# Spectral mixer and gated FFN on one core: T stored in another row order, one transfer where there were two, later T stores spread over more steps, down sums one unit later, modulation rows in pieces

## The chip, the cores and the metric

The kernel runs on one core of a Trainium2 chip. A core has a matrix engine (TensorE, PE in the profile; its weight loads are PEld), VectorE (DVE), ScalarE (ACT), GpSimd (POOL), and SyncE (SP), whose queue issues the transfers between the memory off the core (DRAM here) and the core's own memory of 128 partitions. The transfers themselves are carried by 16 DMA engines. Each engine works through its own instructions in program order and waits on semaphores for the others. The metric is device time in microseconds, from the program's start to its end; lower is better.

## The reference

One block with adaptive layer norm around a spectral mixer (A) and a gated FFN (B), for 8192 tokens of 448 channels in float32. Cut to what matters:

```
sa, ca, ga, sb, cb, gb = (silu(c) @ w_mod) in six rows of 448
h = layernorm(x) * (1 + ca) + sa
z = rfft2(h, over the 8192 tokens)               # complex, in 4 blocks of 112 channels
h = relu(z @ w1 + b1)                            # complex product, per block
o = softshrink(h @ w2 + b2, 0.01)                # complex product, per block
x = x + ga * irfft2(o)
h = layernorm(x) * (1 + cb) + sb
x = x + gb * ((gelu(h @ w_gate) * (h @ w_up)) @ w_down)
```

## The kernel before

The 8192 tokens are taken as 128 by 64, and the transform is done as two short ones. Three parts follow each other.

**Stage A** (lines 130 to 400): x is loaded in 16 pieces `xt` of four columns each, normalised and transformed along the 128 (`dft_a`, L213). The result T, 128 rows (64 frequencies, real and imaginary) by 64 columns by 448 channels, replaces x in `xt` (`out_a`, L218). `store_t` (L355) writes it to DRAM as `td`. The order of the 128 rows is set by the columns of the transform's matrix (`cols` in `_consts`); partition p of `xt` holds the row whose place in a list of four groups (c, 0 to 3) is given by p modulo 4. Pieces 0 to 3 (below `CE`) are stored whole; of pieces 4 to 15 the group c = 0 is stored in stage A, and the 36 remaining stores (the list `late`) are issued during the next stage. `td` has the row order of the partitions, so the four frequencies of a unit lie some rows apart.

**Units** (`step`, L640 on): 32 units, each of four frequencies (`GB`) and half of the channels (224, `HC`). Step i does six things for different units, so that the engines overlap: `fetch_t` loads T of unit i+2 into one of two buffers `tr` (L427: one transfer for the real and one for the imaginary rows, each with 64 columns on the partitions); `stage_s2` does the second transform of unit i on PE (L461 to L463) and ACT and DVE split its result in two f16 parts, `zh` and `zl`; `split_t` splits T of unit i+1 on POOL (`th`, `tl`); `stage_m2`, `stage_m1` are the two products of units i-2 and i-1; `split_y` makes `yh` (ACT) and `yl` (POOL) of unit i-2; `stage_i1` does the first inverse transform of unit i-3 and copies it into one of two buffers `us` (L590), which `store_us` (L607) writes to DRAM as `vd` in two transfers, real and imaginary part. The first two units are fetched by `fetch_first` (columns 0 to 59, from `td`) and `fetch_last` (the last four columns, straight from `xt`, eight transfers of 7 KB). Units 8 and 9 hold frequency 0 and need extra work on POOL, DVE and PE.

Beside this the steps carry work for the FFN, placed by calls of `at(step, hook, ...)`: `load_w` loads 14 pieces of w_gate and w_up into the buffers of `xt` that are free by then (L806: 384 rows; L808: the last 64 rows, twice, onto both halves of the partitions), `squares`, `norms` use them; `load_m`, `down_max`, `down_sums` (POOL, L953 to L956), `store_sums` do seven pieces of w_down; `row_scales` scales the modulation rows. The hooks of a step are called in the order load, pe, act, dve, pool. All transfers are issued by SP in the order in which the program calls them; a transfer that has to wait holds back those behind it.

Ahead of the first unit, `mod_cols`, `dc_cols`, `scale_of` and `mod_row` (L244) turn the modulation into scaled weights w1 and w2.

**FFN** (L970 on): the rest of the inverse transform, read back from `vd` (`load_v`), and the three products of B; nothing there is edited.

The lines that set the two transfers of a unit's result:

```
r = bt * 2 * GB
for ro in range(2):
    dma(vd[h, :, r + ro * GB : r + (ro + 1) * GB], us[ro * 64 : ro * 64 + 64])
```

Of the kernel before, what the change touches and what calls it, by code (L numbers as in the profile page):

```python
# [19 lines left out]
D = 448  # L20
F = 1792
NA, NB, NG = 128, 64, 64
# [28 lines left out]
def spectral_geglu(ctx, tc, x, w1, b1, w2, b2, wg, wu, wd, cvec, wmod, cf1, cs2, cmi, cgm, out):  # L51
# [92 lines left out]
    with ExitStack() as actx:  # L144
# [89 lines left out]
            else:  # L234
                V.scalar_tensor_tensor(ms[:, c], wm[:, k, c], cs[:, k : k + 1], ms[:, c], op0=ALU.mult, op1=ALU.add)

        def mod_row(h, then=lambda: None):

            r = (sb_r, cb_r)[h]
            ps = bank("pd", "psm")  # L240
            for k in range(4):
                if k == 2:
                    then()
                T.matmul(  # L244
                    ps[:, :D], cs[:, k : k + 1].to_broadcast([112, 128]), wn[:, k, h * D : (h + 1) * D], start=k == 0, stop=k == 3
                )
            return lambda: S.copy(r, ps[:, :D])

        ca1 = lp.tile([113, NBLK], F32, name="ca1")
        sa0 = lp.tile([112, NBLK], F32, name="sa0")  # L250
# [100 lines left out]

        def store_t(ch, c=None):

            r = slice(0, 128) if c is None else slice(c, 128, NC)
            dma(td[r, ch * 4 : ch * 4 + 4], xts[ch][r])  # L355


        plan = []
# [43 lines left out]
    with ExitStack() as bctx:  # L402
# [1 line left out]

        tts, trs = {}, {}

        def rows(ri, bt):
            r = BTS.index(bt) * 2 * GB + ri * GB
            p = r % (128 // NC) * NC + r * NC // 128
            return slice(p, p + (GB - 1) * NC + 1, NC)  # L410

        s2s = {}

        def fetch_first(h, ri):
            n = NB - 4
            dma(
                trs[units[h]][0][ri * 64 : ri * 64 + n],
                td[rows(ri, BTS[0]), :n, h * HC : (h + 1) * HC].rearrange("g b c -> b g c"),
            )

        def fetch_last(h, b):
            dma(trs[units[h]][0][NB - 4 + b : 128 : 64], xts[NB // 4 - 1][0 : 2 * GB * NC : NC, b, h * HC : (h + 1) * HC])

        def fetch_t(h, bt):
            raw = bp1.tile([128, GB, HC], F32, tag="tr", name="tr", bufs=2)
            for ri in range(2) if (h, bt) not in units[:2] else ():
                dma(  # L427
                    raw[ri * 64 : ri * 64 + 64],
                    td[rows(ri, bt), :, h * HC : (h + 1) * HC].rearrange("g b c -> b g c"),
                )  # L430
# [53 lines left out]
        def stage_m1(h, bt):  # L484
            zs = ctx_u.pop(("z", h, bt))
            hs = []
            kr = 113
            w = ZW if bt == 0 else GB * 64
            for kk in range(2):
                k = 2 * h + kk  # L490
                zhi, zlo = zs[kk]
                if bt == 0:
                    banks = [bank("pb", "pm1a")[:BS, :w], bank(("pa", "pd")[kk], "pm1b")[:BS, :w]]
                else:
                    ps = bank("pb", "pm1")
# [12 lines left out]
                cnt["h"] += 1  # L508
                hlo = bp.tile([BS, 2, ZW], F16, tag="hl", name="hl", bufs=4)
                if bt == 0:  # L510
                    for ro in range(2):
                        S.activation(hhi[:BS, ro, :w], banks[ro], AF.Relu)
                        V.scalar_tensor_tensor(
                            hlo[:, ro, :w], banks[ro], 0.0, hhi[:BS, ro, :w], op0=ALU.max, op1=ALU.subtract
                        )
                    for ro in range(2):
                        h0 = bp.tile([BS, 1], F32, tag="h0", name="h0", bufs=2)
                        j = slice(ro * NBLK + k, ro * NBLK + k + 1)
                        V.tensor_scalar(h0, banks[ro][:, 0:1], hb[:, j], 0.0, op0=ALU.add, op1=ALU.max)
# [21 lines left out]
        def stage_m2(h, bt, p):  # L541
# [17 lines left out]
            drip()  # L559
            if bt == 0 and p == 0:  # L560

                pn = bank("pb", "pn")
# [39 lines left out]
        def store_us(h, bt, us=None):  # L602

            us = late_us[h, bt] if us is None else us
            r = bt * 2 * GB
            for ro in range(2):
                dma(vd[h, :, r + ro * GB : r + (ro + 1) * GB], us[ro * 64 : ro * 64 + 64])  # L607


        tiny = []  # L610
# [30 lines left out]
        def step(i):  # L641
# [9 lines left out]
            hook("pe")  # L651
            if 1 <= i and i + 1 < nu:
                split_t(*units[i + 1])
            m2 = 0 <= i - 2 < nu
            if m2:
                y = [stage_m2(*units[i - 2], p) for p in range(2)]
# [6 lines left out]
            hook("dve")  # L663
            if 0 <= i - 3 < nu:
                stage_i1(*units[i - 3])
            hook("pool")

        def m2_i1(i, j, el=G):

# [33 lines left out]
        ctx.enter_context(tc.manual_schedule())  # L703
        for u in units[:2]:
            fetch_t(*u)
        for h in range(2):
            for ri in range(2):
                fetch_first(h, ri)
        for h in range(2):
            for b in range(4):  # L710
                fetch_last(h, b)
        zh = [bp1.tile([113, 2, ZW], F16, name=f"zh{i}") for i in range(4)]
        hh_ = [bp1.tile([113, 2, ZW], F16, name=f"hh{i}") for i in range(4)]
        mod_cols()
        bounds1()
        for z in zh:
            S.activation(z[96:113, 0], ones[96:113], AF.Copy, scale=2.0**-ZSC)
        for z in hh_:
            G.tensor_copy(z[96:113, 0], ones[96:113])
        hb_out = dc_cols()  # L720
        scale_of(0, 4, modulated)
        bounds2()
        hb_out()
        weights1()
        row_copy = mod_row(0, lambda: scale_of(1, 13))
        weights2_hi()
        row_copy()
        row_copy = mod_row(1)

        late = [(ch, c) for ch in range(CE, NB // 4) for c in range(1, NC)]  # L730

        def store_late(n):
            for ch, c in late[:n]:
                store_t(ch, c)
            del late[:n]

        store_late(6)

        for u in units[:2]:
            split_t(*u, el=V)  # L740
        row_copy()
# [61 lines left out]
        def load_w(pool, pr, j):  # L803
            wsrc = (wg, wu)[pr][:, j * 256 : (j + 1) * 256]
            raw = raw_tile(pool)
            dma(raw[:, 0:3, :], wsrc[0:384].rearrange("(t p) f -> p t f", p=128))  # L806
            for hh in range(2):
                dma(raw[hh * 64 : hh * 64 + 64, 3, :], wsrc[384:448])  # L808
            return raw

        def squares(pr, j, el=S):
# [151 lines left out]
        for n, i in enumerate([3, 4, 5, 6, 7, 8, 9, 10, 11, 11, 12, 12, 13, 14]):  # L963
            j, pr = divmod(n, 2)
            at(i, "load", pre, npool, ("n", pr, j), load_w, pr, j)
            at(i + 1, "act", squares, pr, j, V if i in (3, 5, 7, 11, 12) and (i < 11 or pr) else S)
            at(i + 2, "pe", norms, pr, j)
            at(i + 2, "pe", norms_out, pr, j)
        for j, i in enumerate([4, 6, 8, 9, 10, 13, 14]):
            at(i, "load", pre, npool, ("m", j), load_m, j)  # L970
            at(i + 1, "dve", down_max, j)
            at(i + 1, "pool", down_sums, j)
            at(i + 2, "load", store_sums, j)
        at(11, "dve", row_scales)
        at(16, "pe", scales1)
        at(16, "pe", scales2)
        for i in range(6):
            at(i, "load", store_late, 5)
        at(1, "act", thresholds)
        for i in range(17):  # L980
            step(i)
# [993 lines left out]
def _consts():  # L1975
# [34 lines left out]
    s2 = s2.reshape(64, 128, 128).transpose(1, 0, 2) * 2.0 ** SSC  # L2010
    s2h = s2.astype(np.float16)
    s2l = (s2 - s2h).astype(np.float16)
    cols = [ri * 64 + bt + NBT * j for bt in BTS for ri in range(2) for j in range(GB)]
    cols = np.array(cols).reshape(NC, 128 // NC).T.reshape(-1)
    rows = np.zeros((128, 2))
    rows[:112, 0], rows[112, 1] = 1, 2.0**-ZSC
# [33 lines left out]
```

## Time and profile before

| | us |
|---|---|
| median of 3 runs (lowest, highest) | 1871.42 (1870.48, 1872.85) |
| the profiled execution | 1873.0 |
| its span in the trace | 1871.0 |
| first matmul of unit 0 (L461) | 81.07 |
| first matmul of unit 31 | 331.90 |
| first and last copy into `us` (L590) start at | 106.1, 354.4 |

In the trace's groups over the stretch 81 to 225 us, the group of DVE's squares (L817) has 5 instructions with a mean of 1435 ns, the group of ACT's squares (L815) 9 with 1048 ns. From step to step the first matmul of a unit comes every 7.5 to 8.2 us, but for steps 9, 10, 11, 13 and 20, which take 13.4, 11.4, 10.0, 10.6 and 10.0 us (from 145.13, 158.54, 169.95, 187.75 and 245.99 us); from 272 us on it is 7.5 us every time. A row of the timeline gives start, length, engine, line, operation and, in brackets, how long the engine sat idle before it and for whom. The table by stretches gives for each stretch the busy time of each engine with its count of instructions, the clock granted to PE, the mean busy share of the 16 DMA engines, and what they moved. The view of the transfers gives the same share in 40 slices, the packets by size, the share of each queue and, below, the transfers issued in the stretch, with KB each.

### The profile page before, as it was taken

How to read it: one execution, taken by the hardware profiler on the slowest of the kernel's cores; microseconds unless marked ns; L12 is line 12 of the kernel's file. 1: busy time of each engine (PE TensorE's matmuls, PEld its weight loads, DVE VectorE, ACT ScalarE, POOL GpSimd, SP SyncE). 2: the span in 40 equal slices, each digit the busy share in tenths (PEclk: the TensorE clock that was granted, in tenths of full speed). 3: DMA queues.
4: the chain of work that ended last, by engine and by line, in shares of the span. 5: the costliest groups of instructions: out<-in, count | busy, mean ns of one | idle time of the engine just before them, and what ended most of it. 6: DMA issues, size and time to landing. Idle time of an engine off the chain costs nothing.

```text
span 1871.0 us, 56475 instructions
## 1 busy us (share of the span) xinstructions
PE 1824.1 (97%) x23352; PEld 1727.0 (92%) x23352; DVE 1415.3 (76%) x2914; ACT 968.4 (52%) x1815; POOL 1318.4 (70%) x1724
## 2 busy tenths in 40 slices
PE   7998999899999999999999999999999999999998
PEld 3697989778898988999999999999999999999998
DVE  8698999887766667777777777777777777777745
ACT  5665678643444444455555555555545554444443
POOL 3377878257777778777777777777777777777534
PEclk9899999999999999999999999999999999999999
DMA  9898878664444445966666666666666666666551
GB/s 355 297 317 235 223 196 226 204 144 104 104 104 104 104 104 124 293 170 170 169 170 169 170 170 170 172 178 178 173 170 172 177 177 177 170 175 174 161 160 55
DMA packets 380613, 330.48 MB, mean 177 GB/s; under 512 B 110784, under 2 KB 358724, under 8 KB 380356
## 3 DMA queue, kind: packets, MB, share of 16 engines
q1 hardware_dynamic: 380356, 326.87, 64.0%
q8 instruction: 183, 3.00, 0.7%
q14 instruction: 74, 0.61, 0.1%
HBM read 243.26 MB, written 60.10 MB: 162 GB/s over the span
## 4 chain that ended last, share of the span: by engine, by line
PE 84%; DVE 5%; DMA 4%; POOL 2%; ACT 2%; issue 1%; SPq 1%; ACTq 0%; POOLq 0%; DVEq 0%
PE set L1485 39%; PE pgu L1242 11%; PE pdn L1315 6%; PE pdn L1317 6%; PE pdn L1316 6%; PE ps L213 2%; PE set L1315 2%; PE set L1317 2%; PE set L1316 2%; DVE y L556 1%; DMA vd<-us 1%; POOL tl L117 1%; POOL yl L117 1%; DMA tr<-td 1%; PE set L1609 1%
## 5 line engine op out<-in xcount | busy, mean ns | idle before, releaser
L1485 PE MATMUL set<-nt,wk 128*128 128x128 f16 x13104 | 736.4, 219 | 3.1 <-ACT sb L1513 1.5
L1485 PEld LDWEIGHTS <-wk 128*128 128x128 f16 x13104 | 733.9, 98 | 3.5 <-issue 2.3
L1317 PE MATMUL pdn<-wd,ac 128*128 128x224 f16 x1218 | 315.5, 259 | 0.6 <-DVE ac L1303 0.6
L1315 PE MATMUL pdn<-wd,ac 128*128 128x224 f16 x1218 | 315.7, 259 | 0.0
L1316 PE MATMUL pdn<-wd,ac 128*128 128x224 f16 x1218 | 315.5, 259 | 0.0
L1242 PE MATMUL pgu<-nt,wk 128*128 128x256 f16 (+1 forms) x2464 | 269.7, 274 | 4.8 <-DVE x L1283 4.8
L1242 PEld LDWEIGHTS <-wk 128*128 128x128 f16 (+1 forms) x2464 | 226.4, 98 | 46.8 <-issue 20.3
L1534 ACT ACTIVATE gl<-c,dg 128x384 f32<-128x384 f32 x168 | 103.5, 616 | 230.2 <-DVE c L1528 227.3
L1560 DVE SCALAR_TENSOR_TENSOR ac<-x,sa_act,ac 128x896 f16<-128x896 f32 x168 | 205.5, 1223 | 20.1 <-ACT ac L1550 20.0
L1291 POOL TENSOR_TENSOR x<-x 128x128 f32<-128x128 f32 x223 | 131.2, 589 | 121.8 <-DVE x L1283 60.9
L1361 POOL TENSOR_TENSOR cq<-cq 128x224 f32<-128x224 f32 x32 | 21.1, 659 | 262.5 <-DVE cq L1360 262.5
L1292 POOL TENSOR_TENSOR x<-x 128x128 f32<-128x128 f32 x223 | 186.4, 836 | 17.5
L1550 ACT ACTIVATE ac<-x,sa_act 128x896 f16<-128x896 f32 x168 | 174.2, 1037 | 14.7 <-POOL x L1294 7.9
L1538 DVE TENSOR_TENSOR x<-c,gl 128x384 f32<-128x384 f32 x168 | 153.3, 912 | 17.2 <-ACT gl L1534 17.0
L1315 PEld LDWEIGHTS <-ac 128*128 128x128 f16 x1568 | 153.4, 98 | 4.9 <-issue 4.8
L1317 PEld LDWEIGHTS <-ac 128*128 128x128 f16 x1568 | 153.4, 98 | 0.8 <-DVE ac L1303 0.8
L1316 PEld LDWEIGHTS <-ac 128*128 128x128 f16 x1568 | 153.5, 98 | 0.1
L1522 DVE TENSOR_TENSOR c<-set,sb 128x512 f32<-128x512 f32 x168 | 115.3, 686 | 35.7 <-PE set L1485 35.6
L1278 ACT ACTIVATE gel<-pgu,dg 128x256 f32<-128x256 f32 x112 | 49.4, 470 | 159.5 <-PE pgu L1242 151.8
L1293 POOL TENSOR_TENSOR x<-x 128x128 f32<-128x128 f32 x223 | 131.7, 591 | 0.0
L1513 ACT COPY sb<-set 128x512 f32<-128x512 f32 x168 | 97.4, 580 | 62.0 <-PE set L1485 60.7
L1294 POOL TENSOR_TENSOR x<-x 128x128 f32<-128x128 f32 x223 | 126.3, 566 | 0.0
(348 smaller groups left out, 3892.3 us busy)
## 6 DMA issues: line engine op xcount, KB each, us to landing
wk<-wk SPq DMA_DIRECT2D x76, 1024.0 KB
wk<-wk SPq DMA_DIRECT2D x76, 768.0 KB
vd<-us SPq DMA_DIRECT2D x64, 224.0 KB
xx<-in_A_x SPq DMA_DIRECT2D x32, 448.0 KB
v<-vd SPq DMA_DIRECT2D x63, 224.0 KB
out<-x SPq DMA_DIRECT2D x31, 448.0 KB
xt<-in_A_x SPq DMA_DIRECT2D x15, 896.0 KB
tr<-td SPq DMA_DIRECT2D x60, 224.0 KB
```

The lines of the kernel that those rows point to most:

```text
L1242: T.matmul(pgu[i, t, q][:, pr * H : (pr + 1) * H], ws[rows, n, w, tw], nts[i][rows, tn, :], start=start, stop=stop, skip_group_check=True,)
L1291: e.tensor_tensor(s1, a21, a22, ALU.add)
L1292: e.tensor_tensor(s2, s1, a11, ALU.subtract)
L1293: e.tensor_tensor(s3, a11, a21, ALU.subtract)
L1294: e.tensor_tensor(s4, a12, s2, ALU.subtract)
L1315: T.matmul(ps, ac[:, 0, ka], w[:, 0, kb], start=n == 0, stop=False)
L1316: T.matmul(ps, ac[:, 0, ka], w[:, 1, kb], start=False, stop=False)
L1317: T.matmul(ps, ac[:, 1, ka], w[:, 0, kb], start=False, stop=n == NP - 1)
L1485: T.matmul(ps2[:, pr, reg * 128 : reg * 128 + 128], slot[:, pr, hl, wt, :], nt[:, xt, :], start=start and j == 0, stop=j == len(terms) - 1 ...
L1538: V.tensor_tensor(xs[u][:, 1::3, :], cts.pop(u)[:, 1], gls.pop(u), ALU.mult)
L1550: S.activation(ac[:, 0], xs[u][:, 0:7], AF.Copy, scale=sa_act[:, t : t + 1])
L1560: V.scalar_tensor_tensor(ac[:, 1], xs.pop(u)[:, 0:7], sa_act[:, t : t + 1], ac[:, 0], op0=ALU.mult, op1=ALU.subtract)
```

## The change

- `cols`: the rows of T stand in another order, frequency by frequency with real and imaginary part side by side, and `store_t` writes `td` in that order (a whole piece as 32 x 4 x 1792, a group as 32 rows in a row). A unit's eight rows then lie together, and `fetch_t` is one transfer of 128 partitions (columns and real or imaginary part) for every unit, the first two too; `rows`, `fetch_first`, `fetch_last` go.
- `store_us` and the last rows of `load_w` are one transfer each instead of two. The destination of the first and the source of the second have a leading dimension of two.
- The 36 later stores of T: three to five in each of the steps 0 to 5 and two or three in steps 6 to 10, instead of six ahead of the units and five in each of the steps 0 to 5; their order is changed so that group c = 1 comes in time.
- `mod_row` takes the pieces k that it is to do; `scale_of(0)` comes ahead of `dc_cols`.
- `down_sums` stands one step later and ahead of `split_y` instead of at the step's end; `store_sums` one step later; `row_scales` at step 13 instead of 11; three of the squares move from DVE to ACT.
- The banks of PSUM of unit 8 and 9's first product change places (`pa`, `pd`), and `pn` takes one of `pd`.

```diff
+        rps = {}
+        def mod_row(h, ks):
+            if h not in rps:
+                rps[h] = bank("pd", "psm")
+            for k in ks:
                 T.matmul(
-                    ps[:, :D], cs[:, k : k + 1].to_broadcast([112, 128]), wn[:, k, h * D : (h + 1) * D], start=k == 0, stop=k == 3
+                    rps[h][:, :D], cs[:, k : k + 1].to_broadcast([112, 128]), wn[:, k, h * D : (h + 1) * D], start=k == 0, stop=k == 3
                 )
...
         def store_t(ch, c=None):
-            r = slice(0, 128) if c is None else slice(c, 128, NC)
-            dma(td[r, ch * 4 : ch * 4 + 4], xts[ch][r])
+            b = slice(ch * 4, ch * 4 + 4)
+            if c is None:
+                dma(td[:, b].rearrange("(c m) b e -> m c b e", c=NC), xts[ch])
+            else:
+                dma(td[c * (128 // NC) : (c + 1) * (128 // NC), b], xts[ch][c:128:NC])
...
-            for ri in range(2) if (h, bt) not in units[:2] else ():
-                dma(
-                    raw[ri * 64 : ri * 64 + 64],
-                    td[rows(ri, bt), :, h * HC : (h + 1) * HC].rearrange("g b c -> b g c"),
-                )
+            r = BTS.index(bt) * 2 * GB
+            dma(raw, td[r : r + 2 * GB, :, h * HC : (h + 1) * HC].rearrange("(g o) b c -> (o b) g c", o=2))
...
-                    banks = [bank("pb", "pm1a")[:BS, :w], bank(("pa", "pd")[kk], "pm1b")[:BS, :w]]
+                    banks = [bank("pb", "pm1a")[:BS, :w], bank(("pd", "pa")[kk], "pm1b")[:BS, :w]]
...
-            for ro in range(2):
-                dma(vd[h, :, r + ro * GB : r + (ro + 1) * GB], us[ro * 64 : ro * 64 + 64])
+            dma(vd[h, :, r : r + 2 * GB].rearrange("b (o g) c -> o b g c", o=2), us)
...
                 split_t(*units[i + 1])
+            hook("pool")
             m2 = 0 <= i - 2 < nu
...
                 stage_i1(*units[i - 3])
-            hook("pool")
...
-        for h in range(2):
-            for ri in range(2):
-                fetch_first(h, ri)
-        for h in range(2):
-            for b in range(4):
-                fetch_last(h, b)
...
-        late = [(ch, c) for ch in range(CE, NB // 4) for c in range(1, NC)]
+        n = NB // 4
+        late = [(ch, c) for ch in range(CE, n - 6) for c in range(1, NC)] + [(ch, 1) for ch in range(n - 6, n)]
+        late += [(ch, c) for ch in range(n - 6, n) for c in range(2, NC)]
...
-        store_late(6)
...
-            for hh in range(2):
-                dma(raw[hh * 64 : hh * 64 + 64, 3, :], wsrc[384:448])
+            dma(raw[:, 3, :], wsrc[384:448].rearrange("(o p) f -> o p f", o=1).to_broadcast([2, 64, 256]))
...
-            at(i + 1, "act", squares, pr, j, V if i in (3, 5, 7, 11, 12) and (i < 11 or pr) else S)
+            at(i + 1, "act", squares, pr, j, V if i in (11, 12) and pr else S)
...
-            at(i + 1, "pool", down_sums, j)
-            at(i + 2, "load", store_sums, j)
-        at(11, "dve", row_scales)
+            at(i + 2, "pool", down_sums, j)
+            at(*((i + 3, "load") if i + 3 < 17 else (16, "dve")), store_sums, j)
+        at(13, "dve", row_scales)
...
-        for i in range(6):
-            at(i, "load", store_late, 5)
+        for i, n in enumerate([3, 4, 4, 4, 5, 5, 2, 2, 2, 2, 3]):
+            at(i, "load", store_late, n)
...
-    cols = [ri * 64 + bt + NBT * j for bt in BTS for ri in range(2) for j in range(GB)]
+    cols = [ri * 64 + bt + NBT * j for bt in BTS for j in range(GB) for ri in range(2)]
```

On SP, from the end of step 3 to the loads of step 4, the transfers stand as follows before the change (destination, source, and the size of the destination's dimensions; `td` are late stores of T, `vd` a unit's result, `tr` the fetch, `s` a constant, `xt` buffers that now take weights):

```order
L355 DMA td<-xt_139 32x1792 x3
L355 DMA td<-xt_140 32x1792 x2
L607 DMA vd<-us 64x896 x2
L427 DMA tr<-td 64x4x224 x2
L435 DMA s_1309<-cs 128x1024
L806 DMA xt_133<-in_B_w_up 128x3x256
L808 DMA xt_133<-in_B_w_up 64x256 x2
L938 DMA xt_134<-in_B_w_down 128x2x448
```

And after it:

```order
L360 DMA td<-xt_135 32x1792
L360 DMA td<-xt_136 32x1792 x3
L593 DMA vd<-us 2x64x896
L417 DMA tr<-td 128x4x224
L422 DMA s_1281<-cs 128x1024
L788 DMA xt_133<-in_B_w_up 128x3x256
L789 DMA xt_133<-in_B_w_up 128x1x256
L919 DMA xt_134<-in_B_w_down 128x2x448
```

Three pairs became single transfers: the fetch with 128 outermost on both sides, the result's store with a 2 ahead of the 64 in the destination (its source has 128 partitions), and the weights' last rows, whose source is 2 x 64 x 256 with a step of 0 in the first dimension.

On POOL, from `split_y` in step 4 to `split_t` in step 6, the first of the down sums (`xt_134`) stands like this before:

```order
L117 TENSOR_TENSOR yl<-y,yh 128x448 x2
L115 CAST th<-tr 128x896
L117 TENSOR_TENSOR tl<-tr,th 128x896
L117 TENSOR_TENSOR yl<-y,yh 128x448 x2
L953 TENSOR_TENSOR xt_134<-xt_134 128x224
L954 TENSOR_TENSOR xt_134<-xt_134 128x224
L955 TENSOR_TENSOR xt_134<-xt_134 128x224
L956 TENSOR_TENSOR xt_134<-xt_134 128x224
L115 CAST th<-tr 128x896
L117 TENSOR_TENSOR tl<-tr,th 128x896
```

And after:

```order
L117 TENSOR_TENSOR yl<-y,yh 128x448 x2
L115 CAST th<-tr 128x896
L117 TENSOR_TENSOR tl<-tr,th 128x896
L117 TENSOR_TENSOR yl<-y,yh 128x448 x2
L115 CAST th<-tr 128x896
L117 TENSOR_TENSOR tl<-tr,th 128x896
L934 TENSOR_TENSOR xt_134<-xt_134 128x224
L935 TENSOR_TENSOR xt_134<-xt_134 128x224
L936 TENSOR_TENSOR xt_134<-xt_134 128x224
L937 TENSOR_TENSOR xt_134<-xt_134 128x224
```

The four sums moved from ahead of a unit's `th` and `tl`, which PE waits for, to behind them.

More of the change, by code (lines that the diff above doesn't have):

```diff
@@ L235, in mod_terms, with row_copy @@
                 V.scalar_tensor_tensor(ms[:, c], wm[:, k, c], cs[:, k : k + 1], ms[:, c], op0=ALU.mult, op1=ALU.add)
[L237 to L243, printed above, removed]
+        rps = {}
[3 more added lines that the diff above has]
+            for k in ks:
                 T.matmul(
-                    ps[:, :D], cs[:, k : k + 1].to_broadcast([112, 128]), wn[:, k, h * D : (h + 1) * D], start=k == 0, stop=k == 3
+                    rps[h][:, :D], cs[:, k : k + 1].to_broadcast([112, 128]), wn[:, k, h * D : (h + 1) * D], start=k == 0, stop=k == 3
                 )
-            return lambda: S.copy(r, ps[:, :D])
+        def row_copy(h):
+            S.copy((sb_r, cb_r)[h], rps[h][:, :D])
         ca1 = lp.tile([113, NBLK], F32, name="ca1")
@@ L405, in spectral_geglu @@
         tts, trs = {}, {}
[L407 to L410, printed above, removed]
         s2s = {}
-        def fetch_first(h, ri):
-            n = NB - 4
-            dma(
-                trs[units[h]][0][ri * 64 : ri * 64 + n],
-                td[rows(ri, BTS[0]), :n, h * HC : (h + 1) * HC].rearrange("g b c -> b g c"),
-            )
-        def fetch_last(h, b):
-            dma(trs[units[h]][0][NB - 4 + b : 128 : 64], xts[NB // 4 - 1][0 : 2 * GB * NC : NC, b, h * HC : (h + 1) * HC])
         def fetch_t(h, bt):
             raw = bp1.tile([128, GB, HC], F32, tag="tr", name="tr", bufs=2)
-            for ri in range(2) if (h, bt) not in units[:2] else ():
-                dma(
-                    raw[ri * 64 : ri * 64 + 64],
-                    td[rows(ri, bt), :, h * HC : (h + 1) * HC].rearrange("g b c -> b g c"),
-                )
+            r = BTS.index(bt) * 2 * GB
+            dma(raw, td[r : r + 2 * GB, :, h * HC : (h + 1) * HC].rearrange("(g o) b c -> (o b) g c", o=2))
             if (h, bt) == units[0]:
@@ L560, in stage_m2 @@
             if bt == 0 and p == 0:
-                pn = bank("pb", "pn")
+                pn = bank("pd", "pn")
                 for kk in range(2):
@@ L714, in spectral_geglu @@
         mod_cols()
+        mod_row(0, (0, 1))
         bounds1()
@@ L719, in spectral_geglu @@
             G.tensor_copy(z[96:113, 0], ones[96:113])
+        scale_of(0, 4, modulated)
         hb_out = dc_cols()
-        scale_of(0, 4, modulated)
         bounds2()
@@ L724, in spectral_geglu @@
         weights1()
-        row_copy = mod_row(0, lambda: scale_of(1, 13))
+        mod_row(0, (2, 3))
+        scale_of(1, 13)
+        mod_row(1, range(4))
         weights2_hi()
-        row_copy()
-        row_copy = mod_row(1)
-        late = [(ch, c) for ch in range(CE, NB // 4) for c in range(1, NC)]
+        row_copy(0)
+        n = NB // 4
+        late = [(ch, c) for ch in range(CE, n - 6) for c in range(1, NC)] + [(ch, 1) for ch in range(n - 6, n)]
+        late += [(ch, c) for ch in range(n - 6, n) for c in range(2, NC)]
         def store_late(n):
@@ L735, in store_late @@
             del late[:n]
-        store_late(6)
         for u in units[:2]:
             split_t(*u, el=V)
-        row_copy()
+        row_copy(1)
         weights2_lo()
```

## The prediction

> **What bounds the kernel now.** I read the page's busy shares first, then the table by stretches, then the chain of waits, then the view of the transfers.
>
> ```profile
> PE 1824.1 (97%) x23352; PEld 1727.0 (92%) x23352; DVE 1415.3 (76%) x2914; ACT 968.4 (52%) x1815; POOL 1318.4 (70%) x1724
> ```
> ```profile
> core 0: us, PE busy (x) PEld busy (x) DVE busy (x) ACT busy (x) POOL busy (x), PEclk, DMA share, GB/s
> 60.00:70.00 10.00, 9.75 (x42) 5.73 (x40) 6.70 (x21) 9.26 (x19) 0.47 (x2) 1.00 1.02 423
> 75.00:75.50 0.50, 0.50 (x2) 0.09 (x2) 0.29 (x2) 0.14 (x1) 0.50 (x1) 0.50 1.09 350
> 107.00:352.00 245.00, 231.23 (x2399) 219.92 (x2398) 225.84 (x457) 176.76 (x325) 190.22 (x189) 0.99 0.85 237
> 272.00:332.00 60.00, 60.00 (x623) 58.77 (x622) 58.76 (x110) 50.57 (x93) 50.73 (x32) 1.00 0.89 232
> ```
>
> PE is busy 97% of the span, and all edits lie ahead of the FFN, so the FFN's time should only shift. In the last row PE has no gap: there a unit costs 60/8 = 7.5 us of PE. But the DMA engines are nearly as full: 0.89 of all sixteen. So the units are bound by PE with little room on the DMA side, as long as the load is spread over sixteen engines. The first two rows give the pace of one engine: 423/16 = 26.4 GB/s for T's 7 KB rows, 350/16 = 21.9 GB/s for the fetch's pieces of 224 floats (896 bytes).
>
> What the change is plainly after are gaps ahead of that. The chain of waits between stage A and the units:
>
> ```profile
> 69.00 4.01 DMA td<-xt
> ...
> 74.49 5.04 DMA tr<-td
> ...
> 79.56 1.65 DMA tr<-xt
> ...
> 81.36 0.95 ACT th L115
> 82.30 0.02 issue
> 82.33 1.09 DVE tl L117
> 83.42 1.19 DVE w2l L322 x2
> 84.61 0.61 DVE zl L470
> ```
>
> And two rows around unit 9, PE and POOL, the bracket being idle time and its cause:
>
> ```profile
> 147.95 0.35 PE L463 MATMUL ps<-s,tl 128*112 128x128 f16 x1 [2.50 <-POOL tl L117]
> ```
> ```profile
> 139.87 0.66 POOL L953 TENSOR_TENSOR xt<-xt 128x224 f32<-128x224 f32 x1
> ...
> 142.08 0.66 POOL L956 TENSOR_TENSOR xt<-xt 128x224 f32<-128x224 f32 x1
> ```
>
> Twelve transfers, the last eight tiny, end at 81.2 us before the second unit can be split; and POOL did four down sums (2.9 us from 139.87 us) ahead of the split that PE's next unit waited for.
>
> **How many engines carry a transfer.** This decides the case, since the store of a unit's result and the weights' last rows now have a leading dimension of two. Three stretches in which little else moves show it:
>
> ```profile
> DMA packets 144, 0.46 MB, mean 199 GB/s; under 512 B 16, under 2 KB 16, under 8 KB 144
> ...
> q1 hardware_dynamic: 144, 0.46, 49.0%
> ...
> out<-x SPq DMA_DIRECT2D x1, 448.0 KB
> ```
>
> This is one store from 128 partitions, 3.5 KB each (435.2 to 437.5 us). It shows 128 data packets and 16 tiny ones, one end per engine. Its packets took 0.490 x 16 x 2.3 = 18.0 us together, so 1.13 us on each of sixteen engines. By size this is the store of one unit's result after the change.
>
> ```profile
> 74.99 5.07 SPq L422 DMA_DIRECT2D tr<-xt  x8
> ```
> ```profile
> DMA packets 10, 0.01 MB, mean 18 GB/s; under 512 B 2, under 2 KB 10, under 8 KB 10
> ```
>
> This is one of the eight 7 KB transfers (80.1 to 80.5 us): two columns' partitions as destination, eight rows as source. It has eight data packets, and two ends: it ran on two engines, though eight rows could have used eight. So the shorter of the two leading dimensions counts.
>
> ```profile
> DMA packets 56, 0.05 MB, mean 54 GB/s; under 512 B 10, under 2 KB 55, under 8 KB 55
> ...
> q1 hardware_dynamic: 55, 0.04, 14.6%
> ```
>
> Here (78.2 to 79.1 us) five of them, issued 0.6 us apart, come out of a backlog at 54 GB/s with 0.146 x 16 = 2.3 engines busy. Had each had another pair, ten engines would have drained them at once. So it is most likely the same pair.
>
> The Trainium skill, page "DMA: Bandwidth & Descriptors", section "Why a DMA increments its semaphore by 16 and not by 1", says that a transfer issued from SP runs on the largest number of engines up to sixteen that divides the slowest dimension, other than one, of both sides, and on the lowest-numbered ones. By that rule a store of 2 x 64 x 896 gets two engines, always the same, and the sum is the one below; without it, if 128 counted, it would be the first rival's. The rows agree for 2 against 8; no row shows 2 against 128.
>
> **The change part by part.** *Store of U* (32 transfers of 448 KB instead of 64 of 224 KB). On two engines each needs 18.0/2 = **9.0 us** of both. Bounds: 8.7 us at 26.4 GB/s for 0.229 MB on each of the two, and 10.5 us at 21.9 GB/s. That is more than the 7.5 us of a unit. And everything else that SP issues also has shares on these two engines and queues behind the stores.
>
> *Weights' last rows* (14 loads, source 2 x 64 x 256): 128 KB on two engines, 64 KB each, is 3.0 us at 21.9 GB/s (2.5 at 26.4), 42 us in all (35).
>
> *Everything else on these engines*:
>
> ```profile
> DMA packets 52272, 59.29 MB, mean 239 GB/s; under 512 B 4764, under 2 KB 44463, under 8 KB 52239
> ...
> vd<-us SPq DMA_DIRECT2D x60, 224.0 KB
> ...
> xt<-in_B_w_up SPq DMA_DIRECT2D x14, 64.0 KB
> ...
> xt<-in_B_w_gate SPq DMA_DIRECT2D x12, 64.0 KB
> ```
>
> From 104 to 352 us 59.29 MB are moved; less 60 x 0.229 and 26 x 0.066 MB, 43.8 MB remain, 2.74 MB per engine. At 21.9 GB/s that is **125 us**, at 26.4 GB/s 104, and by its part (0.74) of the packet time, 0.85 x 248 us, 156. I take 125: 85% of the packets are under 2 KB, as the fetch's are, and the crowding that stretches packets now goes once fourteen engines idle.
>
> *Fetch in one transfer, T's rows in order, later stores spread.* The fetch has 128 on both sides, so sixteen engines; the bytes are the same. SP issues some 70 transfers fewer, and SP's time is not on the path. Spreading the 36 stores only moves bytes within the total. At the start the fetch must now wait for the last store of T too, at most 0.9 us later than 73.0 us (six issues in 5.1 us), but the eight small transfers behind it go: 918 KB at about 215 GB/s are through by 78.5, landed by about 80 instead of 81.2. PE's first half-clock stretch (0.50 above) may get shorter as the first modulation products fill a wait. I take 2 us for the start, bounds 0 and 4.
>
> *Down sums, squares, row scales, banks.* On their own they would fill gaps of PE in steps 8 to 16 (below). With the two engines behind, the waits they remove lie inside the wait for the fetch, and they are worth nothing.
>
> *Does the pair stay busy?* SP issues fetch, loads and store of a step in that order. A unit's copy into `us` waits for the store of two units earlier, as now:
>
> ```profile
> 347.07 3.58 DMA vd<-us
> 350.65 0.03 issue
> 350.68 0.04 ACTq L590
> 350.72 0.33 issue
> 351.05 0.97 ACT us L590 x2
> ```
>
> When a store lands, the next one (9 us) and a fetch stand in the queue already, and the copy and its issue take about 3 us, so the pair does not run dry. PE's chain from a landed fetch to that unit's part (split 2.9 us on POOL, 7.5 us on PE, up to twice that at half clock) fits into the 13 to 18 us that a unit will take. Latency adds nothing; the pair's work sets the end.
>
> ```profile
> 107.12 1.11 SPq L607 DMA_DIRECT2D vd<-us  x2
> ```
> ```profile
> L590 ACT COPY us<-pi x64: 521/534/554, 106.1 to 354.4; 128x448 f32<-128x448 f32 x64
> ```
> ```profile
> 356.08 2.46 SPq L607 DMA_DIRECT2D vd<-us  x4
> ...
> 369.00 0.94 SPq L1030 DMA_DIRECT2D v<-vd  x2
> ```
>
> **Sum.** The first store goes out at 107, less 2 for the start, 105 us. The last unit's copy needs the stores of units 0 to 29: 30 x 9.0 = 270, with 125 and 42 that is 437 us of work on the pair. So the copy ends at about 105 + 437 + 2 = 544 instead of 354.4 + 0.5 = 355 us: **+189 us**. The last two stores follow (18 us and the landing); now 14 us pass from the copy to the read of `vd` at 369, then some 22, of which the first FFN products hide a part: +5. The profiled execution took 1873.0 us, its span 1871.0 and 2.0 around it, so the sum is 2067; the median of the runs is 1.6 below it, which gives **2065 us**. With the low prices (261 + 104 + 35 = 400) it is 2028, with the high store alone (315) 2110, with the high rest alone (156) 2096, with both 2141.
>
> **The rivals.**
>
> *All sixteen engines carry the store after all* (or a pair that changes from transfer to transfer, so that 9 us hide behind two `us` buffers). This is the case that ends faster. Its place is the store of each step, its price per unit 18.0/k us on each of k engines beside 4.2 us (125/30) of other work: it decides at 7.5 us a unit, so from k = 6 up nothing is lost, at 4 there is 8.7 us a unit, at 2 there is 13. Then the gaps count: 2 at the start; 2.5 at unit 9, whose split no longer waits for the sums; about 1 for three squares taken off DVE, the busiest engine of steps 9 to 11; about 2 in steps 12 to 16. That is 1865, bounds 1859 and 1873. Against it: two ends for the 2 against 8. For it: no row with 2 against 128.
>
> *Two engines, but the other transfers pass beside the stores*, each engine serving them in between without loss. Then the stores alone bind: 30 x 9.0 = 270, so 105 + 270 + 2 - 355 = +22, with the tail 5: 1900, 1898 as a median. Against it: shares of packet time near 1 at 423 GB/s say that an engine's time is used up by one packet at a time.
>
> **How the numbers follow.** Two engines, all queued: 0.86. All sixteen or changing pairs: 0.11, of which 0.09 gains over 0.2% and 0.02 is within it. Two engines with the others beside: 0.03. A measurement of this kernel can hardly tell 0.2% (3.7 us) from no change. So faster 0.09, same 0.02, slower 0.89. The range is that of the likeliest case with its bounds, 2028 to 2125, short of 2141, where both high prices would have to come together; the other cases, 0.14, are left out.
>
> **What the profile will show.** If right: from about 105 us on the first matmul of a unit comes every 12 to 20 us, longest in steps 4 to 14, where the weights' last rows come on top; DMA share falls to some 0.35 to 0.45 while `vd<-us` and `tr<-td` fill the chain; PE's busy share in the units falls to about half, with stretches at half clock; landing of a store 9 us and more. The stretch of the FFN is unchanged. Wrong if stores still land in 4 to 6 us with DMA share near 0.85, or if units come every 9 us.

## The result and the profile after

The changed kernel takes 2062.81 us (median of 4 runs, 2061.79 to 2063.56), beside 1872.01 of the kernel before: a ratio of 1.102, 95% interval 1.100 to 1.104. The profiled execution took 2061.8 us, its span 2059.9.

The page of the changed kernel: busy shares, the slices of PE, clock and DMA, and the chain by engine and by line.

```profile
PE 1886.7 (92%) x23352; PEld 1770.1 (86%) x23352; DVE 1413.4 (69%) x2911; ACT 968.4 (47%) x1818; POOL 1317.1 (64%) x1724
...
PE   7976767776499999999999999999999999999999
...
PEclk9987778888699999999999999999999999999999
DMA  9844444445253444459656666566566665665562
...
PE 73%; DMA 18%; DVE 3%; SPq 2%; issue 2%; POOL 1%; ACT 1%; ACTq 0%; POOLq 0%; DVEq 0%
PE set L1466 35%; DMA tr<-td 11%; PE pgu L1223 10%; PE pdn L1296 6%; PE pdn L1298 6%; PE pdn L1297 6%; DMA vd<-us 2%; PE ps L213 2%; PE set L1297 2%; PE set L1296 2%; PE set L1298 2%; DMA xt<-in_B_w_up 1%; DMA raw<-in_B_w_up 1%; PE set L1590 0%; DMA xt<-in_B_w_down 0%
```

The loss lies in slices 3 to 11 (of 51.5 us each, so some 103 to 566 us): there PE stands at 0.6 to 0.7, in the last at 0.4, and the DMA engines at 0.4 to 0.5, at last 0.2. Behind slice 11 PE is back at 0.9 and more. DMA has 18% of the chain, 11% alone the fetch `tr<-td`, which had 1% before. PE is busy 62.6 us longer with the same 23352 matmuls; in the stretch below its granted clock is 0.78, before the change 0.99.

The table by stretches, as in the prediction (clock, DMA share and GB/s stand last), first of the kernel before, then of the changed one:

```profile
104.00:350.00 246.00, 232.23 (x2422) 221.02 (x2420) 226.59 (x458) 177.29 (x326) 190.61 (x190) 0.99 0.85 239
```
```profile
104.00:350.00 246.00, 171.38 (x1435) 152.14 (x1432) 129.77 (x282) 97.89 (x180) 110.75 (x138) 0.78 0.45 149
```

The units' copies of the changed kernel, and a row of the tile `tr` that says how long and how often its readers waited for the fetch, before and after:

```profile
L577 ACT COPY us<-pi x64: 526/542/563, 101.8 to 531.8; 128x448 f32<-128x448 f32 x64
```
```profile
  DMA tr<-td: 2.0, 1
```
```profile
  DMA tr<-td: 126.7, 23
```

The first unit's copy starts 4.3 us earlier than before (101.8 against 106.1), the last one 177.4 us later (531.8 against 354.4). In between, nothing is saturated on the average: DMA moves 149 GB/s at a share of 0.45, and still the split of a unit waits for its fetch, 127 us in all, where it was 2 us.

Why a fetch is late on half-empty engines is seen in a stretch in which only stores of results move (514 to 520 us, view of the transfers):

```profile
DMA packets 88, 0.32 MB, mean 53 GB/s; under 512 B 0, under 2 KB 0, under 8 KB 88
## 3 DMA queue, kind: packets, MB, share of 16 engines
q1 hardware_dynamic: 88, 0.32, 12.8%
```

12.8% of sixteen is 2.05 engines. They move 53 GB/s, so a store of 448 KB (0.459 MB) takes 8.7 us. Two stores are in the queue at that time (issued at 510.2 and 512.0 us); had they different pairs, four engines would be busy. It is the same pair.

The fetches of units 20 to 22 in the chain of waits give the period of a unit:

```profile
325.97 11.81 DMA tr<-td
...
338.51 12.85 DMA tr<-td
...
351.43 11.78 DMA tr<-td
```

One fetch starts 12.5 to 12.9 us after the other, and each is under way for 12 us, though its 0.46 MB would pass in 2 us at the 237 GB/s of before.

What holds it up can be followed packet by packet, since a fetch has 512 packets of 896 bytes and a store 128 of 3584 bytes. The store issued at 324.80 us stands ahead of the first of these fetches, issued at 325.97 us. By the packet records of the trace, the store's packets run from 326.3 to 336.1 us. Of the fetch, 448 packets, fourteen sixteenths, start between 327.0 and 329.3 us, beside the store:

```profile
q1 hardware_dynamic: 631, 0.77, 79.6%
```

(327 to 330 us, view of the transfers.) The other 64, two sixteenths, start between 336.0 and 337.5 us, when the store is through. So it is not that the queue lets one transfer pass at a time, which would cost much the same: fourteen engines serve the fetch at once, and only its share on the store's two engines stands behind the store.

### The profile page after: what moved, and what is told of

Read it like the earlier page. It is cut to its first block, busy times and chain, and to the rows that moved or that the text cites. A ratio compares the mean times of both kernels' runs of the same rounds, so it can differ in the third digit from the quotient of the medians.

```text
span 2059.9 us, 56378 instructions
## 1 busy us (share of the span) xinstructions
PE 1886.7 (92%) x23352; PEld 1770.1 (86%) x23352; DVE 1413.4 (69%) x2911; ACT 968.4 (47%) x1818; POOL 1317.1 (64%) x1724
## 4 chain that ended last, share of the span: by engine, by line
PE 73%; DMA 18%; DVE 3%; SPq 2%; issue 2%; POOL 1%; ACT 1%; ACTq 0%; POOLq 0%; DVEq 0%
PE set L1466 35%; DMA tr<-td 11%; PE pgu L1223 10%; PE pdn L1296 6%; PE pdn L1298 6%; PE pdn L1297 6%; DMA vd<-us 2%; PE ps L213 2%; PE set L1297 2%; PE set L1296 2%; PE set L1298 2%; DMA xt<-in_B_w_up 1%; DMA raw<-in_B_w_up 1%; PE set L1590 0%; DMA xt<-in_B_w_down 0%
## 5 line engine op out<-in xcount | busy, mean ns | idle before, releaser
L1272 POOL TENSOR_TENSOR x<-x 128x128 f32<-128x128 f32 x223 | 130.3, 584 | 152.6 <-DVE x L1264 59.1
L1273 POOL TENSOR_TENSOR x<-x 128x128 f32<-128x128 f32 x223 | 185.7, 833 | 17.5
L117 POOL TENSOR_TENSOR yl<-y,yh 128x448 fp32r<-128x448 f32 x63 | 87.0, 1399 | 71.2 <-ACT yh L115 71.1
L1274 POOL TENSOR_TENSOR x<-x 128x128 f32<-128x128 f32 x223 | 132.4, 594 | 0.0
L543 DVE SCALAR_TENSOR_TENSOR y<-pm,lam,t 64x224 f32<-64x224 f32 x256 | 115.1, 450 | 23.8 <-ACT t L535 19.9
```

Of the source, the lines that this page charges most:

```text
L1272: e.tensor_tensor(s1, a21, a22, ALU.add)
L1273: e.tensor_tensor(s2, s1, a11, ALU.subtract)
L1274: e.tensor_tensor(s3, a11, a21, ALU.subtract)
```

## The experiments

### Undoing the two transfers, one at a time and together

The store alone (first run), the weights' last rows alone (second), both (third), and the store alone put into the kernel before (fourth, the same edit upside down):

```diff
-            dma(vd[h, :, r : r + 2 * GB].rearrange("b (o g) c -> o b g c", o=2), us)
+            for ro in range(2):
+                dma(vd[h, :, r + ro * GB : r + (ro + 1) * GB], us[ro * 64 : ro * 64 + 64])
```
```diff
-            dma(raw[:, 3, :], wsrc[384:448].rearrange("(o p) f -> o p f", o=1).to_broadcast([2, 64, 256]))
+            for hh in range(2):
+                dma(raw[hh * 64 : hh * 64 + 64, 3, :], wsrc[384:448])
```

> The changed kernel, with the store of a unit's result alone back in two transfers of 64 partitions. Theory (two engines carry the whole store and everything queues behind them): the 30 x 9.0 us go from the pair, and only the 14 loads of the weights' last rows stay on it, in steps 3 to 14, where the pair then has 4.2 + 1.1 + 3.0 to 3.5 us of work a unit against 7.5 us of PE; that costs 10 to 30 us, so about 1880 us, between 1865 and 1895. Rival (the fetch from T's new order is slow by itself, since it is the transfer that fills the chain of waits of the changed kernel): still about 2060 us, with tr<-td in the chain.

> The changed kernel, with the weights' last rows alone back in two transfers of 64 rows. Theory: the work of the pair falls by 42 us and rises by 14 x 2 / 16 of that, so -37 us: about 2026 us (2022 to 2035), and the long units of steps 4 to 14 (16 to 19 us now) become as short as those after them (13 us). Rival (the last rows are not on the pair, or pass beside): 2063 us, and steps 4 to 14 stay long.

> The changed kernel with both transfers that have a leading dimension of two undone (store and weights' last rows); T's order, the fetch in one transfer, the spread stores of T, the order of down sums and modulation rows stay. Theory: nothing is left of the loss, and the gaps count as in the prediction's first rival: 1865 us (1859 to 1873). Rival (fetch from T's new order): still near 2060 us. A second rival (the rest of the change costs something of its own): above 1875 us.

> The kernel before, with the store of a unit's result alone made one transfer with a leading dimension of two. Theory: first store at 107 us, then 270 + 125 + 5 us on the pair and 2, so the last copy at about 509 instead of 355 us, and a tail longer by 5 to 12 us: about 2030 us (1995 to 2060). Rival (fetch from T's new order): within 5 us of 1872.

| kernel | median us | ratio to before (95%) | last copy starts, us |
|---|---|---|---|
| before | 1872.14 | | 354.4 |
| store in two | 1876.35 | 1.0023 (1.0013 to 1.0034) | 357.6 |
| last rows in two | 2031.33 | 1.0864 (1.0846 to 1.0882) | 501.5 |
| both in two | 1868.08 | 0.9981 (0.9968 to 0.9993) | 351.6 |
| before, one store | 2041.35 | 1.0915 (1.0898 to 1.0932) | 510.8 |

The rival, that the fetch from T's new order is slow by itself, falls: with both transfers undone that fetch is still there, and the kernel is 4 us faster than before; with the one store put into the kernel before, T's old order is there, and it is 169 us slower. So `tr<-td` in the chain is who suffers, not who causes. The stretch of the third run shows the fetch at ease:

```profile
104.00:350.00 246.00, 232.79 (x2420) 222.89 (x2418) 224.62 (x456) 180.77 (x331) 189.56 (x190) 0.99 0.81 245
```

PE is busy 95% of it again, at the clock 0.99.

The last rows cost 30.3 us at the last copy when the store is on the pair too. Taken off, 14/16 of their work there goes, so 14 loads are 34.6 us, 2.5 us each. They cost 8 us when they have the pair to themselves (1876 against 1868 us), below the 10 to 30 I had expected: of 34.6 us of work on the pair most hides beside PE's 7.5 us a unit.

### Is it the form, or the number of engines?

In the kernel before, each store of 64 partitions is cut in two, at `n` = 32, 62, 57 or 49. All four have 128 transfers of results and the same bytes, and but for the small rest of 2 partitions (7 KB) none has a leading dimension of two.

```diff
             for ro in range(2):
-                dma(vd[h, :, r + ro * GB : r + (ro + 1) * GB], us[ro * 64 : ro * 64 + 64])
+                for b0, b1 in ((0, n), (n, 64)):
+                    dma(vd[h, b0:b1, r + ro * GB : r + (ro + 1) * GB], us[ro * 64 + b0 : ro * 64 + b1])
```

> The kernel before, each store of 64 partitions cut into 32 and 32 (control: four transfers a unit, no leading dimension of two, 32 on both sides). Every theory: sixteen engines carry each, and the time stays within 6 us of 1872.

> The kernel before, each store of 64 partitions cut into 62 and 2: the same number of transfers and bytes as the control, again no leading dimension of two. Theory (the number of engines is the largest one up to sixteen that divides the slower dimensions, and 62 leaves only 2): the whole store is on a pair again, 9.0 us a unit, so as with the one store in the kernel before, 2041 us (2020 to 2060). Rival (it is the form 2 x 64 x 896, or the 448 KB in one transfer, that is slow): as the control, 1872.

> The kernel before, each store of 64 partitions cut into 57 and 7. Theory: 57 leaves three engines, 7 seven: 18.0 x 57/64 / 3 + 18.0 x 7/64 / 7 = 5.6 us a unit on the fullest engines, with 4.2 us of other work 9.8 us against the 7.5 us of PE; the last copy at 107 + 30 x 5.6 + 125 + 5 + 2 = 407 instead of 355 us, with a tail of 5 about 1930 us (1905 to 1950). Rivals: as the control if only a leading dimension of two matters; as the cut into 62 and 2 if any dimension that 16 does not divide goes to two engines.

> The kernel before, each store of 64 partitions cut into 49 and 15. Theory: 49 leaves seven engines, 15 fifteen: 18.0 x 49/64 / 7 + 18.0 x 15/64 / 15 = 2.25 us a unit, with 4.2 us of other work 6.5 us, less than the 7.5 us of PE: no loss beyond some us in crowded steps, 1872 to 1885. Rival (any uneven spread over the engines costs in proportion to it): some (2.25 - 1.1) x 30 = 35 us, about 1907.

The kernel before took 1870.86 us beside these runs.

| cut | engines expected | median us | ratio to before (95%) | last copy starts, us |
|---|---|---|---|---|
| 32 + 32 | 16 | 1881.09 | 1.0050 (1.0035 to 1.0065) | 363.5 |
| 62 + 2 | 2 | 2063.03 | 1.1026 (1.1010 to 1.1043) | 531.8 |
| 57 + 7 | 3 and 7 | 1948.81 | 1.0422 (1.0397 to 1.0446) | 421.8 |
| 49 + 15 | 7 and 15 | 1881.09 | 1.0059 (1.0042 to 1.0076) | 362.8 |

The divisors of the partition count decide, not the form of the transfer. The view of the transfers shows how many engines are busy, in stretches near the end of the units, for 62 + 2 (515 to 530 us) and for 57 + 7 (431 to 436 us):

```profile
q1 hardware_dynamic: 251, 0.76, 12.6%
```
```profile
DMA packets 121, 0.39 MB, mean 78 GB/s; under 512 B 12, under 2 KB 12, under 8 KB 121
## 3 DMA queue, kind: packets, MB, share of 16 engines
q1 hardware_dynamic: 121, 0.39, 19.2%
```

That is 2.0 and 3.1 of sixteen engines. The rule that the prediction drew on (the Trainium skill, page "DMA: Bandwidth & Descriptors", section "Why a DMA increments its semaphore by 16 and not by 1": the largest number up to sixteen that divides the slowest dimension, other than one, of both sides) gives 2 for 62 and 3 for 57. These rows agree with it. Which two engines they are no row here shows.

The last two cuts place the point from which it costs. Seven engines for three quarters of a store cost nothing against the control (1881.09 both): 2.25 + 4.2 us of work a unit is less than the 7.5 us of PE. Three engines cost 58 us at the last copy. The rival that any unevenness costs in proportion is out. Against the sum for 57 + 7 (407 us) the last copy is 15 us late, of which the control's own delay is 9. For 62 + 2 it is 21 us later than with the one store, and the time, 2063 us, lies above the 2020 to 2060 expected; 9 of the 21 us the control has as well, and the cause of the rest stays open.

The control itself missed its expectation: 10 us slower for 64 transfers more. Its units from 296 us on come every 7.9 to 8.9 us instead of 7.5: the control is 1.9 us behind there and 9.1 us at the last copy. SP's own rows name a likely cause. SP's instructions in a unit of the control (start, duration, line, transfer, count):

```profile
314.45 0.40 SPq L909 DMA_DIRECT2D raw<-in_B_w_gate  x1
314.89 1.14 SPq L911 DMA_DIRECT2D raw<-in_B_w_gate  x2
316.07 0.58 SPq L909 DMA_DIRECT2D raw<-in_B_w_gate  x1
316.70 1.14 SPq L911 DMA_DIRECT2D raw<-in_B_w_gate  x2
317.94 2.46 SPq L608 DMA_DIRECT2D vd<-us  x4
320.50 1.27 SPq L427 DMA_DIRECT2D tr<-td  x2
321.87 0.55 SPq L435 DMA_DIRECT2D s<-cs  x1
322.51 0.40 SPq L909 DMA_DIRECT2D raw<-in_B_w_up  x1
```

It issues 13 transfers (not 14, as the expectation further below counts them) in 8.06 us, 0.62 us each, with next to no gap; for the 13 before and the 13 after these it needs 7.53 us. So SP has nothing left beside PE's 7.5 us, and the chain of waits runs through these issues from 314.4 to 317.2 us. The kernel before has 11 there. That SP's issue is what slows the control is the likely reading; no run tried it apart.

### One store on sixteen engines, and the other parts

With both transfers undone 4 us are gained. Three more kernels ask what the rest of the change is worth. The first keeps the store in one transfer, but lays `vd` out so that its slower dimension is 128 (the last rows in two):

```diff
-    vd = dram.tile([2, NB, 128, HC], F32, name="vd")
+    vd = dram.tile([2, 2 * NBT, NB, GB, HC], F32, name="vd")
...
-            dma(vd[h, :, r : r + 2 * GB].rearrange("b (o g) c -> o b g c", o=2), us)
+            dma(vd[h, 2 * bt : 2 * bt + 2].rearrange("o b g c -> (o b) (g c)"), us.rearrange("p g c -> p (g c)"))
...
-                dma(v[:, :, h * HC : (h + 1) * HC], vd[h, i * CB : (i + 1) * CB].rearrange("b q c -> q b c"))
+                for b in range(CB):
+                    dma(v[:, b, h * HC : (h + 1) * HC], vd[h, :, i * CB + b])
...
```

The second has both transfers in two and the down sums back where they were:

```diff
-            at(i + 2, "pool", down_sums, j)
-            at(*((i + 3, "load") if i + 3 < 17 else (16, "dve")), store_sums, j)
-        at(13, "dve", row_scales)
+            at(i + 1, "pool", down_sums, j)
+            at(i + 2, "load", store_sums, j)
+        at(11, "dve", row_scales)
```

(with `hook("pool")` back at the end of a step). The third has both in two and the fetch in two as well:

```diff
-            dma(raw, td[r : r + 2 * GB, :, h * HC : (h + 1) * HC].rearrange("(g o) b c -> (o b) g c", o=2))
+            for ri in range(2):
+                dma(raw[ri * 64 : ri * 64 + 64], td[r + ri : r + 2 * GB : 2, :, h * HC : (h + 1) * HC].rearrange("g b c -> b g c"))
```

> The changed kernel with the rows of vd in another order in memory (blocks of a unit's 128 partitions, so that the store stays one transfer of 448 KB but its slower dimension is 128), the later loads of v in two transfers by batch instead of one, and the weights' last rows in two. Theory: it is the number of engines and not the one transfer that costs: 18.0/16 = 1.1 us a unit on each of sixteen engines, so as with both transfers undone (1868 us), or up to 3 us better for 32 issues fewer on SP: 1863 to 1871. Rival (one transfer of 448 KB delays what is behind it, whatever its engines): 1885 or more.

> The changed kernel with both transfers of leading dimension two undone, and with down sums, their stores and the row scales back where they were before. In the version with the sums moved, PE is 6 us ahead of the kernel before at unit 9 and loses 4 of them in units 10 and 11, where DVE ends PE's waits. Theory (the 2.5 us that the split of unit 9 no longer waits are taken back there): as with the sums moved, 1868 us (1866 to 1870). Rival (the moved sums are worth their 2.5 us): 1870.5 or more. A second rival (they cost POOL time elsewhere): under 1866.

> The changed kernel with both transfers of leading dimension two undone, and with the fetch of a unit in two transfers of 64 partitions from T's new order. In the control with 32 and 32 partitions SP issued 14 transfers in each of the last units at about 0.6 us, 8.4 us a unit, and these units came every 8.1 to 8.7 us. Theory (SP's issue binds only from 12.5 transfers a unit on, 7.5 us / 0.6): here it is 11, so no change, 1868 us (1865 to 1872). Rival (each transfer costs time): the 62 fetches more cost as the control's 60 stores more did, 10 us: 1878.

The kernel before took 1872.47 us beside these.

| kernel | median us | ratio to before (95%) |
|---|---|---|
| one store, 16 engines | 1870.25 | 0.9985 (0.9975 to 0.9996) |
| sums back | 1868.18 | 0.9970 (0.9960 to 0.9980) |
| fetch in two | 1870.55 | 0.9989 (0.9979 to 0.9998) |

One transfer of 448 KB costs nothing when sixteen engines carry it; it then lands after 2.7 us (median):

```profile
vd<-us SPq DMA_DIRECT2D x32, 448.0 KB, 2.7
```

It brings nothing either; a gain by fewer issues isn't seen, and whether reading `v` in twice as many transfers eats one wasn't tried apart. The moved sums are worth nothing, as the theory had it. Where their gain goes, PE's waits from 140 to 190 us show (total, times, longest), first with the sums back, then of the third run above, where they are moved:

```profile
PE pi L573 <- DVE h L506: 3.8, 2, 2.1
PE ps L450 <- POOL tl L117: 2.8, 2, 1.5
PE ps L448 <- DVE h L506: 1.3, 2, 0.7
```
```profile
PE pi L573 <- DVE h L506: 4.3, 2, 2.7
PE ps L448 <- DVE h L506: 2.8, 2, 1.5
```

The 2.8 us of POOL's split are gone, and PE waits 7.1 us for DVE instead of 5.1. Unit 10 starts 2.0 us earlier with the sums moved (152.3 against 154.3 us), unit 11 no longer does (166.2 against 166.1).

The fetch in two took 1870.55 us, inside the expected 1865 to 1872. Its rival was priced too high: the edit adds 32 fetches (64 instead of 32), not 62, and the control paid 10 us for 64, so the rival's time is 1873 and not 1878. The interval ends at 1872.1, below that; but 1870.55 is also 2.4 us above the two kernels with one fetch, and a cost of that size isn't excluded. Eleven transfers a unit fit into 7.5 us or nearly so.

All three beat both kernels, by little. The largest gain is that with the sums back and both doubtful transfers in two, 0.3% (0.2 to 0.4); whether it is really faster than with the sums moved (0.19%, 0.07 to 0.32) isn't shown, since the intervals overlap.

## Why the prediction was right

*What bounds.* PE at 97%, the FFN shifted and not changed: right, as the slices behind 560 us show.

*How many engines.* That the 2 of "2 x 64" counts and not the 128 was an argument from one row, 2 against 8. The cuts by 62 and 57 now show it by itself, and the stretch at 53 GB/s shows the fixed pair. The first rival (all sixteen) and the second (others pass beside, 9 us a unit) are out; the fetches of units 20 to 31 come 12.2 to 13.6 us apart.

*Does the pair stay busy?* Yes, as forecast: of the 428.5 us from the first store's issue to the last wait for a store, fewer than two packets are under way in 1.9 us (packet records of the trace).

*Terms of the sum.* Most are close. That the forecast, 2065 us, came within 3 us of 2062.81 is in part luck, since the last copy came 11.6 us earlier than summed and the tail was 6.5 us longer:

| term, us | predicted | measured | from |
|---|---|---|---|
| first store issued | 105 | 102.8 | SP's rows |
| 30 stores and everything else on the pair | 270 + 125 = 395 | 393.5 | what is left of 428.5 us, from the first issue to the last wait for a store, 512.04 + 19.25 = 531.3 (chain below), less 35 |
| weights' last rows | 42 | 35 | second run |
| last copy ends | 544 | 532.4 | the copies' row |
| tail | +5 | +11.5 | span +188.9, last copy +177.4 |

The weights' rows came out at the lower bound given, 2.5 us each. How the 393.5 us divide isn't settled. In the quiet stretch a store takes 8.7 us, its lower bound, which would be 260 us for the stores and 134 for the rest. In the packet records from 326 to 478 us, where the units run, the twelve stores take 9.1 to 10.4 us from the first packet to the last, 9.8 on average; at that price it would be 293 and 100. Only the sum of the two is shown to be right. In the kernel before, with one store, the same sum gave 509 us for the last copy and it started at 510.8.

*Start.* 2 us were taken, the profile shows 4.3. Over the thirteen profiles the first copy starts at 103.2 us on the average in the seven kernels with the new start (101.8 to 105.2) and at 105.5 in the six with the old one (104.7 to 106.5): 2.3 us. The single profile had a good start.

*Tail.* The place of its wait was missed: the prediction put it at the read of `vd`. The chain around the last copy, and who waited for `us`, after and (last row) before:

```profile
512.04 19.25 DMA vd<-us
531.40 0.97 ACT us L577 x2
...
534.02 5.32 DMA vd<-us
539.35 0.20 ACT g L1152
539.55 14.35 issue
554.13 1.04 ACT pk L1178 x2
...
558.24 9.09 PE pgu L1223 x68
```
```profile
  ACT pk L1178: 14.6, 1
```
```profile
  ACT pk L1197: 0.9, 1
```

The FFN's first cast into `pk` waits until the last two stores have left `us`, 2 x 8.7 us on the pair. The likely reason is that `pk` takes memory that `us` gave up; no run tried it with another place. The prediction let the first FFN products (`pgu`) hide a part of the stores' time; they come behind this cast and hide none of it.

*The profile.* The DMA share (0.45) and the landing of stores (12 and 19 us in the chain) came as forecast. PE's busy share did not: it fell to 0.70 (171.38 of 246 us), not to about half. PE did 59% of the matmuls of before in that stretch (1435 against 2422) but was busy 74% as long: at the granted clock of 0.78 each kept it busy for 0.119 us on average, not 0.096. From unit 6 on the first matmuls of units came 10 to 23.5 us apart, where 12 to 20 were forecast.

*Down sums, squares, row scales, banks*: worth nothing behind the pair, as forecast. Without the pair the first rival gave them and the start 7 us; 4 are there (both undone), 2.3 of them the start's. The step of that rival that failed is the 2.5 us of unit 9, which DVE takes back in units 10 and 11. "SP's time is not on the path" holds for this change (SP issues 872 transfers instead of 958, 86 fewer and not some 70, and has 2% of the chain), but by less than was thought: at 0.58 to 0.62 us an issue, as in the control, twelve or thirteen transfers a unit are the limit by estimate, and the kernel before has eleven.

## What to carry to other kernels

Before two transfers are merged into one, look at the outermost dimension of both sides: a 2 in front, even one with step 0, left two engines here, and cutting 64 as 62 + 2 did the same. What counts is the work on the fullest engine per period against the period of the engine that binds; seven engines were enough here, three were not. When a chain of waits names a transfer on half-empty DMA engines, it may be the victim, as here: look in a quiet stretch for a share that is a small whole number of sixteenths.

## What was not expected of the hardware

SP itself is held up when the pair has much in its queue. SP's rows in the changed kernel:

```profile
103.39 0.41 SPq L417 DMA_DIRECT2D tr<-td  x1
103.89 0.58 SPq L422 DMA_DIRECT2D s<-cs  x1
104.53 3.78 SPq L788 DMA_DIRECT2D xt<-in_B_w_up  x1
108.36 3.34 SPq L789 DMA_DIRECT2D xt<-in_B_w_up  x1
111.75 3.25 SPq L919 DMA_DIRECT2D xt<-in_B_w_down  x1
```

Issues that take 0.4 to 0.6 us take 3.2 to 3.8 behind a store on two engines, also those of transfers that sixteen engines carry. Between 100 and 600 us 69 issues of the changed kernel take more than 2 us, one of the kernel before, and two with both transfers undone. Of a second kind is what the control met: an issue of 0.6 us is small, but thirteen of them fill a unit of 7.5 us (7.5 to 8.1), and with 64 more issues the kernel was 10 us slower.
